# A fused convolution and linear-attention kernel: seven of nine spectral pieces summed by accumulating transfers, epsilon added elementwise, and a new order

## The chip, the cores and the metric

The kernel runs on one core of a Trainium2 chip. The metric is the device time of one execution in microseconds. A core has a tensor engine (TensorE, PE in the profile; its weight loads are PEld), a vector engine (VectorE, DVE), a scalar engine (ScalarE, ACT), GpSimd (POOL) and a queue engine (SyncE, SP) that here only issues transfers. Each engine takes its own instructions in order and waits on semaphores for the others. Transfers run on 16 DMA engines.

## What is computed

Two independent halves, joined along the channels: 2048 positions, 576 channels each.

```python
def _A_ref(q, k, v, shift_k, ssm_k, ssm_D):
    ...
    for t in range(ks):
        k_shift = k_shift + k_pad[:, t:t + S, :] * shift_k[:, ks - 1 - t][None, None, :]
    kv = k_shift * v
    ...
    y_f = kv_f * kf_f[None, :, :, :]
    ...
    y = y + kv * ssm_D[None, None, :]
    return q * y

def _B_ref(x, wqkv, wo):
    ...
    phi = lambda t: jnp.where(t > 0, t + 1, jnp.exp(t)) + 1e-6
    pq, pk = phi(q), phi(k)
    kv = jnp.einsum("bhsd,bhse->bhde", pk, v)
    z = jnp.einsum("bhsd->bhd", pk)
    num = jnp.einsum("bhqd,bhde->bhqe", pq, kv)
    den = jnp.einsum("bhqd,bhd->bhq", pq, z)[..., None] + 1e-6
    o = num / den
    return (lambda x, *d: x.transpose(*d))(o, 0, 2, 1, 3).reshape(B, S, D) @ wo
```

Half A is a short convolution of `k` with four taps, a product with `v`, a long convolution of each channel with its own filter over a transform of 4096 points, and a product with `q`. Half B is linear attention with 32 heads of 18 channels. `phi` is 1e-6 plus a positive function, and that epsilon is the one the change is about.

## The kernel before

**Half A.** The transform is taken in two steps, as matmuls with tables. The channels are cut in three chunks of 192 (`cc`), each of these in three pieces of 64, so there are nine pieces `g`. The filter goes through `h_piece`, `s1` and `s2` first and leaves a spectrum `sph` for each piece, the data (`conv_piece`: `tap`, `tap+`, `tapv`) goes through the same steps and leaves `spu`. In such a tile the partitions alternate between real and imaginary parts: even rows real, odd rows imaginary.

`inv(g, su)` multiplies the two spectra and takes the first inverse step. Two transfers on SP bring the filter's spectrum into `X` with real and imaginary rows swapped. DVE (POOL for one piece) forms two elementwise products, `p2` = `spu` x `X` and `p1` = `spu` x `sph`, in place. These are the four partial products of a complex multiplication, not yet summed. TensorE sums them: for each group `hh` of four channel quads it runs eight 128x128 matmuls at L551, four with `sph` and one table, four with `X` and another, both into the same accumulation. One 128x512 eviction (`i1ev`, to the tile `V`) follows for each group; there are four groups to a piece. `inv2(gi)` takes the second inverse step for three pieces at a time (L576) and multiplies by `q`, either after an eviction to `yb` or straight from PSUM (`i2q`), and stores the result.

**Half B.** `kproj` (L623) and `qproj` (L644) project; `phi` without its epsilon is formed by ACT's exponential and one DVE pass. `b_G` (L673) contracts the keys with the inputs, then come `kv` (L708) and `b_M` (L770), which folds the output weights in. The denominators (`den`, L744 and L748) are inverted, written to DRAM and read back spread over rows (`rb`), and `pqn` multiplies `pqT` by them in place. `b_out` (L813) gives the output. The epsilon that belongs in `phi(q)` is handled by an extra row: `msf` (L798) sums `M` over the rows of each head, times epsilon, into the spare rows 96 to 127 of the last chunk of `M`; two transfers `rh` put the inverse denominators in the same rows of `pqT`.

**The order** of all operations is written out by hand in `PLAN`: a letter for the engine (P TensorE, A ACT, D DVE, G POOL, S SP) and the number of the operation in the order in which the program records them. `PLACES` gives every buffer its address. So each engine's queue is fixed. Operations marked `two` have two tensors in SBUF as input; one of them on POOL is given a wait on the last one on DVE that stands before it in `PLAN`:

```python
            if o.info.get("two"):
                if o.eng == "DVE":
                    last = ins
                elif last is not None:
                    tc.add_manual_dep(ins, last.name, mybir.DependencyInfo(mybir.DependencyClass.Sync, mybir.DependencyReason.SCHED_ONLY),
                                      reason="products of VectorE and GpSimd one after the other")
```

The copy helper has the lines L229 (ACT), L231 (DVE) and L233 (POOL), the two-tensor helper is L236, and SP's transfers are L222.

Of the kernel before, what the change touches and what calls it, by code (L numbers as in the profile page):

```python
# [13 lines left out]
S = 2048  # L14
D = 576
# [9 lines left out]
HDT = []  # L25
ACC = [(0, 1), (2, 1)]
# [88 lines left out]
def _tables():  # L115
# [11 lines left out]
    E = np.empty((128, 32 + 2, 128), np.float32)  # L127
# [3 lines left out]
    W = np.zeros((32, 3, 32), np.float32)  # L131
    for bb in range(16):
        for k1 in range(16):
# [5 lines left out]
            W[16 + bb, 0, 2 * k1 + 1] = c  # L139
            W[2 * k1, 1, 2 * bb] = c  # L140
# [8 lines left out]
    for i in range(2):  # L149
        E[:, 32 + i, :] = np.kron(np.eye(4), W[:, 1 + i, :])  # L150

# [17 lines left out]
    C[:, o:o + 8] = EPS  # L169
# [14 lines left out]
def kernel(  # L184
# [49 lines left out]

    def tt(e, o, a, b, op):
        return (nc.vector if e == "DVE" else nc.gpsimd).tensor_tensor(out=o, in0=a, in1=b, op=op)  # L236
# [10 lines left out]
    Esb = SB("Esb", [128, 34, 128], side=1)  # L247
# [31 lines left out]
    for f in range(2):  # L279
        P.op("G", lambda e, f=f: nc.gpsimd.memset(pqT[f].t[64:128, 4, :], 0.0), wr=[(pqT[f], (4, g)) for g in (2 * f, 2 * f + 1)] + [(pqT[f], "r")], name="pqz", ms=1024, st="pqz%d" % f)  # L280
# [4 lines left out]
    load("cst", cst, lambda e: dma(e, cst.t[:], C_d), 256 * Ct.shape[1], 1612)  # L285
    load("srow", srow, lambda e: dma(e, srow.t[:], A_shift_k.rearrange("(p d) j -> p d j", p=64)), 4608, 72, engs=EARLY)
# [4 lines left out]
    load("Esb", Esb, lambda e: dma(e, Esb.t[:].rearrange("p a c -> p (a c)"), E_d), 1114112, 8704)  # L291
# [194 lines left out]
    def s2(C, cc, pp, nm):  # L486
# [23 lines left out]
        for kh in range(4):  # L510
            ps = psb(1, "s2ps")

            def mm(e, kh=kh, ps=ps):
                for j in range(4):
                    nc.tensor.matmul(  # L515
                        ps.t[32 * j:32 * j + 32, 0, :],
                        lhsT=W2()[32 * kh:32 * kh + 32, :], rhs=ct.t[32 * kh:32 * kh + 32, 8 * j:8 * j + 8],
                        start=True, stop=True)
            P.op("P", mm, rd=[ct, idw], wr=[ps], name="s2" + nm, st=st, mm=[(512, 32, 32)] * 4)
            P.op("AD", lambda e, kh=kh, ps=ps: copy(  # L520
                e, view(sp.t[:], 32 * kh, [[256, 8], [128, 2], [1, 32]]), ps.t[:, 0, :].rearrange("p (w k t) -> p w t k", w=8, t=2)),
                 rd=[ps], wr=[(sp, kh)], name="s2ev" + nm, n=512, st=st)
# [134 lines left out]
    for g in range(4):  # L657
        for c in range(5):
            qproj(c, g)
# [295 lines left out]
```

## Time and profile before

| what | us |
|---|---|
| median of 3 runs | 160.37 (159.92 to 160.57) |
| profiled execution, first to last instruction (span) | 158.3 |
| TensorE busy | 149.8 |
| DVE busy | 141.8 |
| ACT busy | 125.1 |
| POOL busy | 59.6 |

Of the profiled execution the page gives the span alone, not a time of its own; the median run is 2.07 us above it. A table of stretches has, per row, the stretch, its length, and for each engine in the order PE, PEld, DVE, ACT, POOL the busy time and the number of instructions; then the granted TensorE clock, the DMA engines' busy share and GB/s. A group of instructions has the line, engine, operation, output and inputs, shapes and count, then the busy time and the mean duration of one, then idle time before. A row of the chain of waits or of a timeline begins with its start and its length in us. A row of waits has who waited, for whom, the us in total, the number of times and the longest.

### The profile page before, as it was taken

To read this page: it belongs to the slowest core of one execution; us is meant where nothing else is said; L and a number is where in the kernel's file an instruction comes from. 1 tells how busy PE (TensorE), PEld (TensorE's weight loads), DVE (VectorE), ACT (ScalarE), POOL (GpSimd) and SP (SyncE) were. 2 spreads that over 40 slices of the span, in tenths; PEclk is the share of its full clock that TensorE was granted. 3 is DMA by queue.
4 is the path that set the end of the run, shared out by engine and by line. 5 is a ranking of instruction groups with operands and counts; after the bars stand their busy time and mean duration, and the time that the engine had idled before them with its cause. 6 is when DMAs were issued, how large, how long until landed. Compare 5 with 4: busy or idle time off the path is not lost.

```text
span 158.3 us, 4158 instructions
## 1 busy us (share of the span) xinstructions
PE 149.8 (95%) x1663; PEld 118.6 (75%) x1663; DVE 141.8 (90%) x170; ACT 125.1 (79%) x229; POOL 59.6 (38%) x53
## 2 busy tenths in 40 slices
PE   6899999999999999999999999999999999999960
PEld 2478885535679888788888887877767799999960
DVE  1547999999999998999999999999989999999690
ACT  4038999999996566467559699999899999998760
POOL 8801310011163554603611999799290000001520
PEclk9999999999999999999999999999999999999997
DMA  5999939999999809965546867881463599405766
GB/s 146 283 384 313 245 79 299 284 187 239 352 384 259 299 15 333 377 270 103 99 131 214 159 149 209 312 288 63 178 232 112 173 331 361 143 4 147 188 181 160
DMA packets 26317, 34.37 MB, mean 217 GB/s; under 512 B 15802, under 2 KB 20923, under 8 KB 25530
## 3 DMA queue, kind: packets, MB, share of 16 engines
q1 hardware_dynamic: 25754, 32.54, 66.6%
q0 software_dynamic: 544, 1.57, 5.6%
q8 instruction: 13, 0.21, 0.7%
q14 instruction: 6, 0.05, 0.1%
HBM read 20.86 MB, written 4.99 MB: 163 GB/s over the span
## 4 chain that ended last, share of the span: by engine, by line
PE 78%; ACT 8%; DVE 6%; DMA 2%; issue 1%; SPq 1%; DVEq 0%; ACTq 0%
PE ps_all L813 13%; PE ps_all L623 12%; PE ps_all L673 12%; PE ps_all L644 11%; PE ps_all L467 8%; PE ps_all L551 8%; PE ps_all L515 5%; ACT sph L229 3%; PE ps_all L576 3%; ACT V L229 3%; DMA x_sb<-in_B_x_dram 2%; PE ps_all L436 2%; DVE Ch L231 2%; ACT yb L229 1%; PE ps_all L708 1%
## 5 line engine op out<-in xcount | busy, mean ns | idle before, releaser
L644 PE MATMUL ps_all<-xT,wq 128*126 128x512 bf16 (+1 forms) x100 | 23.8, 381 | 0.1
L813 PE MATMUL ps_all<-M,pqT 126*128 126x288 bf16 (+1 forms) x160 | 22.5, 287 | 0.0
L623 PE MATMUL ps_all<-wk,xT 128*128 128x288 bf16 x160 | 20.4, 286 | 0.4 <-DVE xT L231 0.4
L402 DVE TENSOR_TENSOR m<-kh,Wj 128x6144 bf16<-128x6144 bf16 x6 | 20.1, 3349 | 0.0
L229 ACT ACTIVATE Cu<-ps_all 128x768 bf16<-128x768 f32 x22 | 17.3, 856 | 3.2 <-PE ps_all L467 3.2
L623 PEld LDWEIGHTS <-xT 128*128 128x128 bf16 x160 | 17.4, 110 | 3.1 <-DVE xT L231 0.6
L236 POOL TENSOR_TENSOR pqT<-pqT,rb 126x1024 bf16<-126x1024 bf16 (+1 forms) x9 | 19.1, 2174 | 1.0 <-DVE v L236 1.0
L813 PEld LDWEIGHTS <-pqT 126*128 126x128 bf16 (+1 forms) x160 | 16.6, 110 | 3.7 <-issue 1.9
L644 PEld LDWEIGHTS <-wq 128*126 128x126 bf16 (+1 forms) x100 | 12.5, 131 | 8.7 <-issue 2.2
L229 ACT ACTIVATE V<-ps_all 128x512 bf16<-128x512 f32 x32 | 17.2, 624 | 1.8 <-PE ps_all L551 1.8
L628 ACT ACTIVATE ek<-ps_all,neg 128x576 bf16<-128x576 f32 x16 | 11.9, 743 | 8.3 <-PE ps_all L623 8.3
L467 PEld LDWEIGHTS <-Gsb 128*128 128x128 bf16 x192 | 16.1, 98 | 2.6 <-issue 1.6
L551 PE MATMUL ps_all<-Esb,sph 128*128 128x128 bf16 x144 | 17.9, 219 | 0.1
L551 PE MATMUL ps_all<-Esb,X 128*128 128x128 bf16 x144 | 17.9, 219 | 0.0
L236 POOL TENSOR_TENSOR m<-m 128x1536 bf16<-128x1536 bf16 x4 | 12.4, 3096 | 13.1 <-DVE m L236 8.9
L673 PE MATMUL ps_all<-pk,x_sb 128*128 128x289 bf16 (+1 forms) x128 | 17.1, 287 | 0.0
L229 ACT ACTIVATE sph<-ps_all 128x512 bf16<-128x512 f32 x30 | 16.6, 608 | 0.2
L229 ACT ACTIVATE Ch<-ps_all 128x768 bf16<-128x768 f32 x19 | 15.2, 853 | 1.0 <-PE ps_all L467 0.8
L229 ACT ACTIVATE spu<-ps_all 128x512 bf16<-128x512 f32 x28 | 15.1, 613 | 0.6 <-PE ps_all L515 0.6
L236 POOL TENSOR_TENSOR q<-yb,q 128x384 bf16<-128x384 bf16 x4 | 3.6, 912 | 29.4 <-DVE yb L231 27.6
L673 PEld LDWEIGHTS <-x_sb 128*128 128x128 bf16 x128 | 12.3, 98 | 2.9
L551 PEld LDWEIGHTS <-sph 128*128 128x128 bf16 x144 | 14.0, 98 | 0.5 <-DVE sph L236 0.2
(96 smaller groups left out, 301.9 us busy)
## 6 DMA issues: line engine op xcount, KB each, us to landing
X<-sph SPq DMA_DIRECT2D x18, 256.0 KB
v<-in_A_v_dram SPq DMA_DIRECT2D x2, 1152.0 KB
out_dram<-ob SPq DMA_DIRECT2D x16, 144.0 KB
q<-in_A_q_dram SPq DMA_DIRECT2D x1, 2304.0 KB
out_dram<-q SPq DMA_DIRECT2D x12, 192.0 KB
rb<-r_scr SPq DMA_DIRECT2D x8, 252.0 KB
x_sb<-in_B_x_dram SPq DMA_DIRECT2D x3, 576.0 KB
kh<-in_A_k_dram SPq DMA_DIRECT2D x1, 1584.0 KB
```

Source lines behind the costliest of these rows:

```text
L229: nc.scalar.activation(out=o, in_=i, func=ACTF.Copy)
L236: return (nc.vector if e == "DVE" else nc.gpsimd).tensor_tensor(out=o, in0=a, in1=b, op=op)
L402: return nc.vector.tensor_tensor(out=m.t[:], in0=i0, in1=i1, op=ALU.mult)
L467: nc.tensor.matmul(ps.t[:, bank, lo - 384 * bank:hi - 384 * bank], lhsT=Gsb.t[:, b, ri, :], rhs=src[:, lo - CC * j:hi - CC * j], start=Tru ...
L515: nc.tensor.matmul(ps.t[32 * j:32 * j + 32, 0, :], lhsT=W2()[32 * kh:32 * kh + 32, :], rhs=ct.t[32 * kh:32 * kh + 32, 8 * j:8 * j + 8], st ...
L551: nc.tensor.matmul(ps.t[:, 0, 128 * c:128 * c + 128], lhsT=src.t[:, 4 * hh + c, :], rhs=Esb.t[:, 32 + wi, :], start=(wi == 0), stop=(wi == 1))
L576: nc.tensor.matmul(ps.t[:, 0, n * j:n * j + n], lhsT=Esb.t[:, 2 * b + ri, :], rhs=V[gi].t[:, 2 * b + ri, :], start=(ri == 0), stop=(ri == 1))
L623: nc.tensor.matmul(ps.t[:, hh, 0:HALF], lhsT=cols(xT.t[0:KT[t], t, :], r), rhs=wk.t[0:KT[t], t, HALF * hh:HALF * hh + HALF], start=(t == 0 ...
L628: P.op("A", lambda e: nc.scalar.activation(out=eb.t[:], in_=ps.t[:, :, 0:HALF], func=ACTF.Exp, bias=neg1.t[:]), rd=[ps, neg1], wr=[eb], na ...
L644: nc.tensor.matmul(ps.t[0:hn, 0, :], lhsT=wq.t[0:KT[t], t, h0:h0 + hn], rhs=xT.t[0:KT[t], t, :], start=(t == 0), stop=(t == 4))
L673: nc.tensor.matmul(ps.t[0:m, 0, 0:n], lhsT=x4[r // 4].t[:, r % 4, :] if t == 4 else x_sb[r // 4].t[:, r % 4, 128 * t:128 * t + 128], rhs=p ...
L813: nc.tensor.matmul(ps.t[:, 0, 0:HALF], lhsT=cols(pqT[r // 8].t[0:kn, c, 512 * (r // 4 % 2):512 * (r // 4 % 2) + 512], r), rhs=M.t[0:kn, c, ...
```

## The change

In seven of the nine pieces (`ZA`) the sum of the four partial products is formed before TensorE sees them. `X` now gets the odd (imaginary) rows of `sph` in all rows, and a third transfer fills the odd rows of `sph` with its even ones. POOL multiplies `X` by a column of signs, -1 and +1 by turns (`sgn`). After the two products, two transfers issued by POOL add `X`, rows swapped, into `sph` (`zacc`, accumulating). A quad then needs one matmul instead of two. Pieces 7 and 8 stay as they were.

In half B the extra rows, `msf`, its copy, `rh` and their memsets are gone. Instead epsilon is added to every element of `pqT` (`pqe`) after the denominators have been formed and before `pqn`.

The last two groups of the second three pieces in `inv2` (`gi == 1 and bg >= 6`) take the other way to the product with `q`, with a store each. `PLAN` and `PLACES` are new throughout. The options `MS2`, `MI1`, `MO`, `MQ` and `ZP` are off or empty, and the code for them does what it did.

```diff
+ZP = []
+ZA = [0, 1, 2, 3, 4, 5, 6]
+NW = 1 if len(ZP) + len(ZA) == 9 else 3
+MS2, MI1, MO, MQ = False, False, False, False
...
+    C[0::2, o + 4] = -1.0
+    C[1::2, o + 4] = 1.0
+    C[:, o + 5] = -C[:, o + 4]
...
+    def scale(e, o, a, c):
+        if e == "ACT":
+            nc.scalar.activation(out=o, in_=a, func=ACTF.Copy, scale=c)
+        else:
+            (nc.vector if e == "DVE" else nc.gpsimd).tensor_scalar(out=o, in0=a, scalar1=c, scalar2=None, op0=ALU.mult)
...
+        z, za = g in ZP or g in ZA, g in ZA
         for i in range(2):
-            load("X", xb, lambda e, i=i: dma(e, xb.t[i:128:2], tx.t[1 - i:128:2]), 262144, 4096, rd=[tx], wr=[(xb, i)])
+            load("X", xb, lambda e, i=i: dma(e, xb.t[i:128:2], tx.t[(1 if z else 1 - i):128:2]), 262144, 4096, rd=[tx], wr=[(xb, i)])
+        if z:
+            load("X", tx, lambda e: dma(e, tx.t[1:128:2], tx.t[0:128:2]), 262144, 4096, wr=[tx])
...
+        if z:
+            P.op("GDA", lambda e: scale(e, xb.t[:], xb.t[:], sgn.t[:, int(za):int(za) + 1]), rd=[sgn], wr=[xb], name="sgn", n=2048, st=st)
...
+        if za:
+            for i in range(2):
+                load("zacc", tx, lambda e, i=i: nc.gpsimd.dma_start(out=tx.t[i:128:2], in_=xb.t[1 - i:128:2], accum_op=ALU.add),
+                     262144, 4096, rd=[xb], wr=[(tx, 2 * i), (tx, 2 * i + 1)], engs="G")
...
+                        for wi, src in ((0, tx),) if z else ((1, tx), (2, xb)):
+                            nc.tensor.matmul(ps.t[:, hh, 128 * c:128 * c + 128], lhsT=src.t[:, 4 * (h0 + hh) + c, :], rhs=Esb.t[:, 32 + wi, :],
+                                             start=(wi < 2), stop=(wi != 1))
...
+            ya = gi in YA and not (gi == 1 and bg >= 6)
...
+            P.op("DG", lambda e, c=c, hn=hn, f=f: (nc.vector if e == "DVE" else nc.gpsimd).tensor_scalar(
+                out=pqT[f].t[0:hn, c, :], in0=pqT[f].t[0:hn, c, :], scalar1=EPS, scalar2=None, op0=ALU.add),
+                 wr=[(pqT[f], (c, g)) for g in (2 * f, 2 * f + 1)], name="pqe", n=1024)
...
-        load("rh", None, lambda e, f=f: dma(e, pqT[f].t[96:128, 4, :], ap(r_d, 1024 * f, [[2 * S, 32], [1, 1024]])), 65536, 2048,
-             rd=[(rtok, (f, 0))], wr=[(pqT[f], "r")])
-    P.op("G", lambda e: nc.gpsimd.memset(M.t[64:128, 4, :], 0.0), wr=[(M, 4), (M, "s")], name="Mz", ms=576)
...
-    P.op("P", smm, rd=[(M, c) for c in range(5)] + [cst], wr=[sps], name="msf", mm=[(288, 126, 128)] * 10)
...
```

In the new order the engines of some operations differ too:

| operations | before | after |
|---|---|---|
| `sgn` | none | POOL 7 |
| `zacc` | none | POOL 14 |
| `pqe` | none | POOL 9, DVE 1 |
| `pqn` | POOL 9, DVE 1 | POOL 8, DVE 2 |
| `tap+` | DVE 6, POOL 4 | DVE 8, POOL 2 |
| `i1ev` | ACT 32, DVE 4 | ACT 29, DVE 7 |
| `oev` | ACT 22, DVE 10 | ACT 25, DVE 7 |
| `X` on SP | 18 | 25 |

On POOL the seven sign passes stand apart: piece 3's among the convolution's products, pieces 5 and 0 among and after `pqn`, piece 4's after that, then six `zacc` (pieces 3, 5, 4), the sign passes of pieces 6, 2 and 1, and eight `zacc` (pieces 6, 2, 1, 0).

More of the change, by code (lines that the diff above doesn't have):

```diff
@@ L246 @@
     Gsb = SB("Gsb", [128, 16, 2, 128], side=1)
-    Esb = SB("Esb", [128, 34, 128], side=1)
+    Esb = SB("Esb", [128, 32 + NW, 128], side=1)
+    sgn = SB("sgn", [128, 2], FP32, side=1)
     srow = SB("srow", [64, D // 64, 4])
@@ L657 @@
     for g in range(4):
-        for c in range(5):
-            qproj(c, g)
+        for c, m in ((0, 2), (2, 2), (4, 1)) if MQ else [(c, 1) for c in range(5)]:
+            qproj(c, m, g)
     GT = SB("GT", [128, 5, D])
```

213 lines of the change are left out of this document (109 added, 104 removed), and 32 rows, old and new, of the table PLACES.

## The prediction

> **What bounds the kernel now.** I read the page's busy shares first, then TensorE's own waits, then a table of stretches, then the chain that ended last.
>
> ```profile
> PE 149.8 (95%) x1663; PEld 118.6 (75%) x1663; DVE 141.8 (90%) x170; ACT 125.1 (79%) x229; POOL 59.6 (38%) x53
> PE 78%; ACT 8%; DVE 6%; DMA 2%; issue 1%; SPq 1%; DVEq 0%; ACTq 0%
> ```
> ```profile
> PE ps_all L844 <- DVE cft L840: 1.5, 1, 1.5
> PE ps_all L323 <- DVE x L231: 0.5, 1, 0.5
> PE ps_all L623 <- DVE xT L231: 0.4, 1, 0.4
> ```
> ```profile
> 75.00:100.00 25.00, 24.73 (x256) 20.46 (x254) 24.60 (x27) 19.95 (x33) 16.39 (x8) 1.00 0.65 167
> 100.00:124.00 24.00, 24.00 (x317) 17.78 (x317) 22.68 (x32) 22.91 (x50) 14.61 (x6) 1.00 0.53 187
> 124.00:150.00 26.00, 25.92 (x400) 24.93 (x392) 24.55 (x31) 23.83 (x52) 2.65 (x3) 1.00 0.59 196
> ```
>
> TensorE is busy for 149.8 of 158.3 us, at the full granted clock in these stretches (1.00, the column before the DMA share), and every wait it has lies in the first microseconds. From 75 us to 150 us it has no gap to speak of, so matmul time taken away there is time taken off, until another engine is late. The busy columns are PE, PEld, DVE, ACT, POOL: DVE and ACT run within 1 to 2 us of TensorE in the last two stretches. Only POOL and the DMA engines have room (2.65 of 26 us; share 0.53 to 0.59). So the question is which engine is late next.
>
> The span is 158.3 us; the median of the runs is 160.37. I make the sum on the span and carry the difference, 2.07 us, over.
>
> **What TensorE loses.** Two rows of the chain and the two groups give the price.
>
> ```profile
> 99.58 1.30 PE ps_all L798 x10
> 128.60 2.68 PE ps_all L551 x48
> ```
> ```profile
> L551 PE MATMUL ps_all<-Esb,sph 128*128 128x128 bf16 x144 | 17.9, 219 | 0.1
> L551 PE MATMUL ps_all<-Esb,X 128*128 128x128 bf16 x144 | 17.9, 219 | 0.0
> ```
>
> Matmuls are pipelined, so the mean of 219 ns is not what one occupies: 48 in a row take 2.68 us, 55.8 ns each. Each piece has 16 on `sph` and 16 on `X`; seven pieces lose the 16 on `X`: 112 x 0.0558 = 6.25 us. The ten matmuls of the epsilon row (L798) go too: 1.30 us, with a copy, two small transfers and three memsets behind them that hold nothing up. Together 7.55 us: the span would be 150.75 us, a run 152.8.
>
> **What ACT and DVE have.** The new order moves a net eight copies onto ACT. The costliest form is the 128x768 eviction, so at most 8 x 0.86 = 6.9 us over the whole span:
>
> ```profile
> L229 ACT ACTIVATE Cu<-ps_all 128x768 bf16<-128x768 f32 x22 | 17.3, 856 | 3.2 <-PE ps_all L467 3.2
> ```
>
> From 100 to 150 us ACT is already busy for 22.91 + 23.83 = 46.7 of 50 us, and the change takes no eviction away: a quad of the inverse still needs its whole copy. If nothing moved between the stretches, ACT alone would let these 50 us shrink by only 3.3, to a run of 157.1. I take that as a cross-check, not a term, since the order may move copies into ACT's free 5 us before 100. DVE has eight instructions fewer and is not the bound unless it is held up (second rival).
>
> **What POOL gets.** Per piece a pass over `X` by a column of signs (`sgn`, 2048 elements, one tensor in) and two accumulating transfers (`zacc`, 256 KB each); ten passes that add epsilon to `pqT` (`pqe`, 1024 elements), nine on POOL. None of these is in the trace. The nearest rows:
>
> ```profile
> L280 POOL MEMSET pqT<- 64x1024 bf16 x2 | 1.9, 947 | 0.1
> L277 POOL MEMSET x<- 128x256 bf16 x4 | 1.2, 305 | 0.1
> L233 POOL COPY x<-x_sb 128x256 bf16<-128x256 bf16 x1 | 0.4, 395 | 0.0
> L236 POOL TENSOR_TENSOR pqT<-pqT,rb 126x1024 bf16<-126x1024 bf16 x7 | 15.0, 2172 | 1.0 <-DVE v L236 1.0
> L236 POOL TENSOR_TENSOR X<-spu,X 128x2048 bf16<-128x2048 bf16 x1 | 4.1, 4074 | 2.8 <-DVE spu L231 2.8
> L407 POOL DMA_DIRECT2D m<-m x2 | 2.5, 1274 | 12.2 <-DVE m L402 6.7 <-DVE zsel L729 5.5
> ```
> ```profile
> DMA to landing us min/median/max: 6.4/6.5/6.5
> ```
> ```profile
> q0 software_dynamic: 272, 0.79, 44.3%
> ```
> ```profile
> 103.14 0.35 SPq L222 DMA_DIRECT2D Esb<-tab_e  x1
> ```
>
> A pass with one input lies between a memset (0.95 us for 1024 elements) and one with two inputs (2.17 us; 4.07 for 2048). It is nearest to the copy, 395 against 305 ns for the memset of that size, 1.3 times: 0.95 to 1.23 us for `pqe`, 1.9 to 2.45 for `sgn`. I take 1.1 and 2.15. The Trainium skill (GPSIMD Engine Reference, 3.1 Elementwise — side-by-side cycle accounting) has a short loop body bound at 1.03 cycles per element of a 1.2 GHz clock; by that estimate `sgn` is 1.8 us and the chain below 2.1 us shorter; no row here shows it.
>
> Issuing an accumulating transfer of 768 KB held POOL for 1.27 us; SP issues a plain one in 0.35. `zacc` is a third of that size: 0.35 to 1.34, taken 0.9. It landed 6.5 us after issue; the queue's 0.79 MB took 44.3% of a 10 us stretch, 4.43 us of all engines, so 2.1 us are fixed and 256 KB takes 1.48: landing after 3.6 us, with 6.5 as the other end.
>
> **Whether POOL keeps up.** POOL and TensorE run in order, and in the new order both can be counted between two places: the end of the denominators (`den`), which frees `pqT` for `pqe`, and the inverse matmuls of piece 1, which wait for its `zacc`. POOL has 9 `pqe`, 1 `acc`, 8 `pqn`, 6 `sgn`, 1 product and 12 `zacc`: 9.9 + 1.27 + 17.4 + 12.9 + 4.07 + 10.8 = 56.3, and 3.6 to land: 59.9 us. For TensorE:
>
> ```profile
> 79.66 1.98 PE ps_all L673 x16
> 81.64 0.33 PE ps_all L467 x4
> 93.92 1.39 PE ps_all L708 x25
> 97.92 0.65 PE ps_all L770 x4
> 112.42 0.99 PE ps_all L515 x28
> 127.98 0.62 PE ps_all L813 x5
> 142.39 0.33 PE ps_all L576 x4
> ```
>
> 7 groups of L673 (13.9), 22 of L467 (7.3), 48 of L515 at four matmuls (6.8), L708 (1.4), 5 of L770 at two (1.6), 26 of L813 (16.1), inverse quads 17 x 4 and 8 x 8 matmuls (7.4), 7 of L576 (2.3): 56.8 us. POOL is late by 3.1 us, and TensorE stalls by it at the last pieces: everything behind, the output matmuls woven in among them included, waits in TensorE's queue. With the lower ends POOL needs 50.5 us and nothing is late; with the copy's rate, 1.34 and 6.5 it needs 71.2 and is 14.4 late; with two-input rates 89, which the copy row speaks against.
>
> SP's seven extra `X` transfers (the third of a piece must wait until the first two have read the tile, and what is behind it on SP waits too: output stores and `q`) are apart from their pair in the order; at nothing, as the loads run a stage ahead.
>
> **The transfers themselves.**
>
> ```profile
> q1 hardware_dynamic: 1531, 3.96, 54.6%
> 126.34 0.39 SPq L222 DMA_DIRECT2D q<-in_A_q_dram  x1
> ```
>
> The first row is of 120 to 140 us: 3.96 MB in 10.9 us of all engines, 363 GB/s. From 100 to 150 us the engines are used for 0.53 x 24 + 0.59 x 26 = 28 us. The change adds 14 x 1.48 = 20.7 and 7 x 0.72 = 5: 54 in 50 us. The 2.36 MB of `q` alone, 6.5 us, come in amid the `zacc`. So a `zacc` will at times be served by halves; between 0 and 6.5 us, taken 1.9.
>
> **Sum:** 158.3 - 7.55 + 3.1 + 1.9 = 155.75; with 2.07, 157.8 us. The start of the new order is dealt differently, but the same loads come first, and its end has one more product straight out of PSUM and one more store, with DVE off the chain there for most of it: 0 for both, give or take 1. Two sums of the convolution come from POOL to DVE, whose eight fewer instructions pay for them.
>
> **Rivals.** (1) *All of it is hidden.* POOL at its lower ends: 152.8. ACT's 46.7 of 50 us speak against. 10%.
>
> (2) *POOL's one-input passes and DVE's two-tensor passes shut each other out.* The trace keeps the two kinds apart:
>
> ```profile
> 57.22 3.12 POOL L236 TENSOR_TENSOR v<-m,v 128x1536 bf16<-128x1536 bf16 x1 [3.71 <-DVE m L402]
> 97.85 2.12 POOL L236 TENSOR_TENSOR pqT<-pqT,rb 126x1024 bf16<-126x1024 bf16 x1
> ```
> ```profile
> 60.79 1.75 DVE L236 TENSOR_TENSOR m<-m 128x3072 bf16<-128x3072 bf16 x1
> 99.95 0.95 DVE L236 TENSOR_TENSOR v<-m,v 128x1536 bf16<-128x1536 bf16 x1
> 118.86 1.22 DVE L236 TENSOR_TENSOR sph<-spu,sph 128x2048 bf16<-128x2048 bf16 x1
> ```
>
> The two POOL passes end at 60.34 and 99.97, where DVE's begin; in the code they carry a mark (`two`), which `sgn` and `pqe` lack. So no row shows them side by side. If they exclude each other, six `sgn` meet DVE's products (1.22 us) and five `pqe` its conv passes; meeting halfway, 6 x 0.6 = 3.6 and about 3.3 more on POOL's late chain: 161.4 to 164.7, say 163. It decides from 3.4 us on. 27%. The Trainium skill (SBUF — State Buffer, Who interferes with whom) states just this: a VectorE instruction with two SBUF inputs contends with a GpSimd instruction that reads SBUF, and the second one blocks; with it the sum is this rival's.
>
> (3) *POOL is slow*: 14.4 us late: 158.3 - 7.55 + 14.4 + 2.07 = 167.2. 13%.
>
> (4) *Given back*: POOL's and the transfers' lateness adds to about 7.5, and the time stays at 160.4. 13%.
>
> **How the numbers follow.** 157.8 has 37% (155.5 to 159.5). What differs by under 0.5% from 160.37 a measurement of this kernel can't tell from no change. Faster: 37 + 10 = 47%; same 13%; slower 27 + 13 = 40%. The range reaches from just above the first rival to short of the third: 153.5 to 166. The forecast's own is 155.5 to 159.5, as cases of both signs hold much of the chance.
>
> **What would show it.** L551's successor down to 176 matmuls and TensorE busy near 142 us; `sgn` near 2.15 us and `pqe` near 1.1; TensorE waiting for DMA `sph` in the last 30 us, about 5 us in all (right), or for nothing (first rival). DVE passes on `sph` and `X` longer than 1.22 us, or POOL passes of twice their shortest, show the second. I am wrong in kind if ACT stands where I have POOL.

## The result, and the profile after

| | before | after |
|---|---|---|
| time, median | 160.30 us | 206.22 us (204.57 to 208.83, 4 runs); 205.99 of the three compared |
| profiled execution, its span | 158.3 us | 202.5 us |
| granted clock, mean | 0.994 | 0.898 |

Some executions of one and the same kernel take over 1.5% longer than its fastest; the ratios and the comparisons below leave these out, and the table of experiments has the medians with and without them.

The ratio is 1.2831 (95% interval 1.2776 to 1.2886): some 46 us slower. The prediction said 157.8 us, in a range of 153.5 to 166. It was wrong in direction and far outside its range.

The page of the changed kernel: busy time by engine, the granted clock in 40 slices, and the group of the epsilon passes (busy time in all, mean ns of one; the last column says what the engine waited for):

```profile
PE 156.6 (77%) x1541; PEld 117.0 (58%) x1541; DVE 160.4 (79%) x164; ACT 127.8 (63%) x237; POOL 131.8 (65%) x79
PEclk9999999999999999999995555855799999599999
...
L821 POOL TENSOR_SCALAR pqT<-pqT 126x1024 bf16<-126x1024 bf16 (+1 forms) x9 | 28.6, 3179 | 2.9 <-PE ps_all L788 2.3
```

TensorE was forecast near 142 us. It has 122 matmuls fewer than before and is busy for 6.8 us more, because for a good part of the second half its clock is granted at 0.5: the same matmuls take longer. And it idles for 46 us, where before it idled for 8.5. POOL has gone from 59.6 to 131.8 us. The groups apart by shape:

```profile
L250 POOL TENSOR_SCALAR X<-X,sgn 128x2048 bf16<-128x2048 bf16 x7 | 40.8, 5843 | 1.1 <-PE ps_all L810 1.1
L253 POOL TENSOR_TENSOR pqT<-pqT,rb 126x1024 bf16<-126x1024 bf16 x6 | 13.6, 2277 | 1.2 <-issue 1.2
L576 POOL DMA_DIRECT2D sph<-X x14 | 12.3, 1190 | 2.7 <-DVE X L253 1.4 <-issue 1.3
L253 DVE TENSOR_TENSOR X<-spu,X 128x2048 bf16<-128x2048 bf16 x8 | 19.5, 2441 | 0.3 <-POOL X L250 0.3
L589 PE MATMUL ps_all<-Esb,sph 128*128 128x128 bf16 x144 | 13.9, 229 | 12.3 <-DVE ob L242 7.0 <-issue 2.7 <-ACT ob L240 1.1
L589 PE MATMUL ps_all<-Esb,X 128*128 128x128 bf16 x32 | 5.7, 265 | 0.0
```
```profile
DMA to landing us min/median/max: 3.7/6.0/8.6
```

`sgn` takes 5.84 us (forecast 2.15), `pqe` 3.18 (forecast 1.1): POOL's new work is 28.6 + 40.8 + 12.3 = 81.7 us, where the forecast's prices make 37.5. All of the difference is in the passes: issuing the transfers took 12.3 us, forecast 14 x 0.9 = 12.6. An accumulating transfer lands 6.0 us after its issue (forecast 3.6). The mean of VectorE's products on `X` has doubled from 1.21 to 2.44 us, and the mean hides how. Their shortest, median and longest, in ns:

```profile
L253 DVE TENSOR_TENSOR X<-spu,X x8: 1211/1221/4727, 148.5 to 178.9; 128x2048 bf16<-128x2048 bf16 x8
```

Most take 1.22 us as before; three, which lie beside POOL's sign passes, take 4.3 to 4.7. The 144 + 32 inverse matmuls are the 176 forecast. Where the waits went (engine and line, what it waited for, us in all, times, the longest):

```profile
PE ps_all L484 <- DVE v L253: 20.1, 1, 20.1
DVE ct L523 <- POOL pqT L253: 14.4, 1, 14.4
PE ps_all L589 <- DVE ob L242: 7.0, 3, 3.4
```

One wait of TensorE is 20.1 us long. The second row tells whose it is: VectorE stands for POOL. POOL's own timeline (start, length, what):

```profile
79.44 29.18 POOL L821 TENSOR_SCALAR pqT<-pqT 126x1024 bf16<-126x1024 bf16 x9 [2.34 <-PE ps_all L788]
108.68 1.23 POOL L424 DMA_DIRECT2D m<-m  x1
...
156.01 18.59 POOL L250 TENSOR_SCALAR X<-X,sgn 128x2048 bf16<-128x2048 bf16 x3
174.56 5.29 POOL L576 DMA_DIRECT2D sph<-X  x6
180.44 1.73 POOL L576 DMA_DIRECT2D sph<-X  x2 [0.59 <-DVE X L253]
```

From 79.44, where the prediction's chain begins, to piece 1's `zacc` at 179.85 us POOL has hardly a gap: 100.4 us, 4.4 of them idle, for which the forecast had 56.3. The stretches (busy columns PE, PEld, DVE, ACT, POOL; then the clock, the DMA share, GB/s):

```profile
100.00:104.00 4.00, 2.62 (x26) 1.95 (x24) 0.00 (x0) 3.65 (x6) 3.86 (x3) 1.00 0.42 120
104.00:125.00 21.00, 2.24 (x15) 1.45 (x15) 10.83 (x7) 1.32 (x2) 19.64 (x9) 0.56 0.54 152
125.00:150.00 25.00, 24.00 (x250) 12.35 (x249) 19.24 (x24) 18.99 (x38) 23.17 (x7) 0.69 0.63 234
150.00:180.00 30.00, 20.89 (x235) 17.27 (x234) 29.50 (x21) 18.20 (x42) 28.51 (x15) 0.89 0.80 221
```

From 104 to 125 us POOL is busy almost throughout, VectorE for half of it, TensorE and ACT hardly at all. In the next 25 us TensorE looks fully busy, but at a clock of 0.69. Of the chain that ended last (start, length, what), three pieces stand out:

```profile
163.87 4.30 DVE X L253
...
169.66 4.29 DVE X L253
...
177.53 6.80 DMA sph<-X
```

The first two are held products on `X`; VectorE's evictions `ob`, for which TensorE waits 7.0 us in all, come behind them in its queue. The third is the landing of an accumulating transfer.

### The profile page after: what moved, and what is told of

Read it like the earlier page. It is cut to its first block, busy times and chain, and to the rows that moved or that the text cites. A ratio compares the mean times of both kernels' runs of the same rounds, so it can differ in the third digit from the quotient of the medians.

```text
span 202.5 us, 3962 instructions
## 1 busy us (share of the span) xinstructions
PE 156.6 (77%) x1541; PEld 117.0 (58%) x1541; DVE 160.4 (79%) x164; ACT 127.8 (63%) x237; POOL 131.8 (65%) x79
## 3 DMA queue, kind: packets, MB, share of 16 engines
q0 software_dynamic: 1664, 5.24, 14.1%
## 5 line engine op out<-in xcount | busy, mean ns | idle before, releaser
L250 POOL TENSOR_SCALAR X<-X,sgn 128x2048 bf16<-128x2048 bf16 x7 | 40.8, 5843 | 1.1 <-PE ps_all L810 1.1
L240 ACT ACTIVATE Cu<-ps_all 128x768 bf16<-128x768 f32 x23 | 18.4, 848 | 23.4 <-PE ps_all L484 21.6
L821 POOL TENSOR_SCALAR pqT<-pqT 126x1024 bf16<-126x1024 bf16 (+1 forms) x9 | 28.6, 3179 | 2.9 <-PE ps_all L788 2.3
L484 PE MATMUL ps_all<-v,Gsb 128*128 128x192 bf16 x96 | 11.2, 265 | 21.4 <-DVE v L253 20.1
L841 PE MATMUL ps_all<-M,pqT 126*128 126x288 bf16 (+1 forms) x160 | 25.5, 309 | 0.1
L589 PE MATMUL ps_all<-Esb,sph 128*128 128x128 bf16 x144 | 13.9, 229 | 12.3 <-DVE ob L242 7.0
L419 DVE TENSOR_TENSOR m<-kh,Wj 128x6144 bf16<-128x6144 bf16 x6 | 22.8, 3818 | 0.1
L523 DVE STREAM_TRANSPOSE ct<-Cu 128x1024 f32<-128x1024 f32 x9 | 10.7, 1220 | 14.4 <-POOL pqT L253 14.4
L841 PEld LDWEIGHTS <-pqT 126*128 126x128 bf16 (+1 forms) x160 | 17.1, 114 | 6.5 <-issue 3.3
L253 DVE TENSOR_TENSOR X<-spu,X 128x2048 bf16<-128x2048 bf16 x8 | 19.5, 2441 | 0.3 <-POOL X L250 0.3
L253 POOL TENSOR_TENSOR hT<-hT,Drow 1x64 bf16<-1x64 bf16 (+2 forms) x5 | 1.7, 342 | 27.5 <-DVE hT L242 10.3
L240 ACT ACTIVATE spu<-ps_all 128x512 bf16<-128x512 f32 x30 | 17.3, 621 | 2.8 <-PE ps_all L534 2.1
L253 POOL TENSOR_TENSOR pqT<-pqT,rb 126x1024 bf16<-126x1024 bf16 (+1 forms) x8 | 17.2, 2297 | 1.2 <-issue 1.2
L713 PE MATMUL ps_all<-pk,x_sb 128*128 128x289 bf16 (+1 forms) x128 | 17.1, 287 | 0.0
```

Of the source, the lines that this page charges most:

```text
L240: nc.scalar.activation(out=o, in_=i, func=ACTF.Copy)
L250: (nc.vector if e == "DVE" else nc.gpsimd).tensor_scalar(out=o, in0=a, scalar1=c, scalar2=None, op0=ALU.mult)
L419: return nc.vector.tensor_tensor(out=m.t[:], in0=i0, in1=i1, op=ALU.mult)
L484: nc.tensor.matmul(ps.t[:, bank, lo - 384 * bank:hi - 384 * bank], lhsT=Gsb.t[:, b, ri, :], rhs=src[:, lo - CC * j:hi - CC * j], start=Tru ...
L589: nc.tensor.matmul(ps.t[:, hh, 128 * c:128 * c + 128], lhsT=src.t[:, 4 * (h0 + hh) + c, :], rhs=Esb.t[:, 32 + wi, :], start=(wi < 2), stop ...
L713: nc.tensor.matmul(ps.t[0:m, 0, 0:n], lhsT=x4[r // 4].t[:, r % 4, :] if t == 4 else x_sb[r // 4].t[:, r % 4, 128 * t:128 * t + 128], rhs=p ...
```

## The experiments

Four things could hold the 46 us: POOL's passes, their meeting with VectorE's, the transfers of the sums, and the new order itself. The measured times in one table: the median of all 4 to 6 runs (one run for e1 and e2), then the median of the runs compared. The expectations name the first.

| run | base | edit | us, all runs | us, compared |
|---|---|---|---|---|
| e1 | after | `pqe` on VectorE | 195.95 (one run) | |
| e2 | after | `sgn` on VectorE | 197.56 (one run) | |
| e3 | after | both | 184.49 | 182.65 |
| e4 | after | neither pass at all | 178.35 | 178.18 |
| e5 | e3 | no `zacc` | 175.09 | 173.64 |
| e6 | e5 | no third copy of X | 175.19 | 174.22 |
| e7 | e3 | old sums | 174.60 | 174.60 |
| e8 | e3 | 26 idle matmuls | 182.98 | 180.70 |
| e9 | after | `acc` earlier | 208.03 | 208.03 |
| e10 | before | epsilon elementwise on VectorE | 169.84 | 169.70 |
| e11 | before | new sums | 198.69 | 193.50 (one run) |
| e12 | e7 | no `pqe` | 174.63 | 174.27 |
| e13 | after | a buffer freed earlier | 205.86 | 205.86 |
| e14 | e7 | 26 idle matmuls | 172.54 | 171.91 |
| e15 | before | as e10, placed earlier | 164.75 | 164.75 |
| e16 | e12 | `wv` loaded earlier | 172.87 | 172.40 |
| e17 | e16 | 21 idle matmuls | 182.83 | 182.00 |

### The passes on POOL: e1, e2, e3, p1

A letter of the order names an engine: G is POOL, D is VectorE. e1 changes it for the nine `pqe`, e2 for the seven `sgn`, e3 for all sixteen.

```diff
-... D265 G264 P211 A212 D70 A213 P494 G267 G241 ...
+... D265 D264 P211 A212 D70 A213 P494 D267 D241 ...
```

> The changed kernel with its nine epsilon passes on DVE instead of POOL, at the same places of the order; nothing else is moved. Theory A (a pass of one input on POOL is simply long, 2.77 us for 1024 elements, and what is queued behind it on POOL comes late): 9 x 2.77 = 25 us leave POOL's queue ahead of the second `acc`, TensorE's wait of 20 us for the convolution goes, and the time falls to 175 to 183 us. Theory B (POOL's passes are of the length I forecast, and the time goes into POOL and DVE shutting each other out): only the 3.7 us that these passes are longer than their shortest and what DVE loses beside them come back, 193 to 198 us. Theory C (the accumulating transfers are what is late): no change here, above 200.

> The changed kernel with its seven sign passes on DVE instead of POOL; the epsilon passes stay on POOL. Theory A: the stall of 20 us behind the epsilon passes stays, the 6 x 5.44 us of signs in POOL's queue go: 183 to 190 us. Theory B: DVE's products on `X`, longer by 9.8 us in all, come back to 1.21 us each, 194 to 198 us. Theory C: `zacc` lands 6.0 us after issue as before and TensorE still waits for it at the last pieces, above 200.

> Both kinds of passes on DVE, POOL keeps the transfers, `pqn` and its sums. Theory A and B: no one-input pass is left on POOL, and the time is that of my sum without POOL's lateness plus 7 to 10 us more work on DVE: 156 to 164 us. Theory C: TensorE waits for `sph` by transfer in the last pieces, 170 us or more.

195.95 and 197.56 lie in B's ranges, 184.49 (ratio 1.1367, 1.1328 to 1.1406) in C's. The two gains, 10.0 and 8.4, add to 18.4, and together they give 23.3. So POOL's passes are some 23 us of the loss, and 22 are left that none of the three names rightly. The two profiles bear out a part of A and a part of B: TensorE's wait for `v` is 4.5 us in e1 and 17.1 in e2, as A has it, and in e2 all products on `X` are back at 1.22 us, as B has it.

p1 measures single passes, one at a time and then two engines side by side; it computes nothing of the kernel, and its output is zeros. POOL's copies and passes with an immediate number have VectorE's memsets beside them; its pass by a column and its products run with VectorE idle.

```text
POOL alone: copy; tensor_scalar (immediate, column); tensor_tensor
DVE alone: tensor_scalar (column); tensor_tensor
together: POOL 3 tensor_scalar || DVE 12 products
          POOL 2 copies || DVE 6 products
          POOL 2 tensor_scalar || DVE 8 tensor_scalar
```

> None of the reference's work: the output is zeros, and one pass of each kind runs by itself and then beside a pass of the other engine. Alone on POOL, 128 partitions. Theory A: a multiply or an add by one number takes 2.7 ns per element alone (5.4 us for 2048, 2.8 for 1024), a copy 1.2 ns (2.4 us) and a two-input product 2.0 ns (4.07). Theory B: the multiply takes 2.1 us alone and 5 only beside DVE's products. Both: a DVE product that starts beside a POOL pass takes up to that pass's length instead of 1.2 us if the two exclude each other, 1.2 us if they do not. The sign pass on DVE should take 0.6 to 1.2 us, on ACT 1.7 to 2.1.

Its timeline, POOL first, then VectorE; all of 2048 elements:

```profile
8.75 1.89 POOL L46 COPY b<-a 128x2048 bf16<-128x2048 bf16 x1
23.04 5.44 POOL L49 TENSOR_SCALAR b<-a,col 128x2048 bf16<-128x2048 bf16 x1 [4.09 <-DVE colb L41]
28.56 4.04 POOL L50 TENSOR_TENSOR b<-a,c 128x2048 bf16<-128x2048 bf16 x1
32.69 3.60 POOL L51 TENSOR_TENSOR b<-a,colb 128x2048 bf16<-128x2048 bf16 x1
...
45.75 6.46 POOL L60 TENSOR_SCALAR e<-c,col 128x2048 bf16<-128x2048 bf16 x1 [9.47 <-ACT c L58]
...
58.21 5.82 POOL L62 TENSOR_SCALAR e<-c,col 128x2048 bf16<-128x2048 bf16 x1
...
82.10 5.86 POOL L73 TENSOR_SCALAR l<-k 128x2048 bf16<-128x2048 bf16 x1 [5.03 <-DVE k L72]
88.05 5.67 POOL L74 TENSOR_SCALAR l<-k 128x2048 bf16<-128x2048 bf16 x1
```
```profile
36.32 0.75 DVE L53 TENSOR_SCALAR d<-b,col 128x2048 bf16<-128x2048 bf16 x1 [13.45 <-POOL b L51]
37.57 1.23 DVE L55 TENSOR_TENSOR d<-d,b 128x2048 bf16<-128x2048 bf16 x1
45.68 25.25 DVE L64 TENSOR_TENSOR f<-c,g 128x2048 bf16<-128x2048 bf16 x12 [4.50 <-ACT c L58]
82.04 15.87 DVE L76 TENSOR_SCALAR f<-k 128x2048 bf16<-128x2048 bf16 x8
```

A sign pass alone on POOL takes 5.44 us, more than a product of two tensors (4.04) and nearly three times a copy (1.89). Written as a product with a column spread over the row (L51) it took 3.60. VectorE does the pass in 0.75. So theory A is right about the length. The meeting is real, too: twelve products that take 12 x 1.23 = 14.8 us alone took 25.25 beside three POOL passes, so they lost 10.5 us to passes that last 6.46 + 2 x 5.82 = 18.1. They were not all slowed: nine took their own 1.23 us, and three, one beside each POOL pass, 4.62. Beside two copies on POOL (2.95 and 2.77 us in place of 1.89) six products took 10.66 us in place of 7.4. Eight fast one-input passes, some 6 us alone, took 15.87, and 4.2 of these lie behind the end of POOL's second pass at 93.72: hardly more than two got through beside POOL's two. How the 23 us divide between the passes' length and the meeting, no run separates.

### TensorE's wait of 20 us: e9, e13

The first reading was POOL's queue: the convolution's second accumulating transfer (`acc`, whose product was ready at 91.8 us) stood behind the `pqe` until 108.68. e9 moves that one word.

```diff
-G244 D83 G250 G261 G247 G270 G258 S259 G84 ...
+G244 D83 G84 G250 G261 G247 G270 G258 S259 ...
```

> The new kernel (206.2 us) with one word of the order moved: the second accumulating transfer of the convolution (acc) goes to POOL ahead of five of the passes that add epsilon instead of behind them, right behind the product that it sums. All the passes stay on POOL. Theory Q (TensorE's wait of 20 us at 104 to 124 us is POOL's queue: the transfer was ready at 92 us and issued at 108.7): issued at 92 to 95 us, the wait shrinks to under 8 us, and the time falls to 190 to 198 us. Rival (POOL's sum of work sets the end, wherever the transfer stands): 203 to 208 us.

It was issued at 95.52, and nothing was gained: 208.03 us, TensorE's wait 20.3. VectorE's timeline in e9 shows why:

```profile
99.79 1.22 DVE L523 STREAM_TRANSPOSE ct<-Ch 128x1024 f32<-128x1024 f32 x1
115.32 1.25 DVE L523 STREAM_TRANSPOSE ct<-Cu 128x1024 f32<-128x1024 f32 x1 [14.30 <-POOL pqT L253]
116.48 5.39 DVE L253 TENSOR_TENSOR m<-m 128x1536 bf16<-128x1536 bf16 x1
```

A transpose of the convolution's spectrum has no data from `pqT`. What it waits for is memory: its output `ct` is placed over two `rb` tiles, which POOL's normalisations (`pqn`) still have to read, and those stand behind POOL's `pqe`. The convolution's sum (L253 on `m`) is next in VectorE's queue and takes 5.39 us in place of 0.92, beside POOL's sign pass. e13 lets POOL do the two `pqn` in question first, with their `pqe`, and `acc` ahead of them; nothing is added.

```diff
-P494 G267 G241 A495 ... G244 D83 G250 G261 G247 G270 G258 S259 G84 ... G263 ... G272 G260
+P494 G267 G261 G270 A495 ... D83 G84 G263 G272 G241 G244 G250 G247 G258 S259 ... G260
```

> The new kernel (206.2 us) with POOL's passes in another order, none added or taken away: the two normalisations whose reciprocals (rb) lie where VectorE's next transpose (ct) is to be written, and their two epsilon passes, go ahead of the other five epsilon passes, and the second accumulating transfer of the convolution ahead of them. Theory B (TensorE's wait of 20 us is this buffer: VectorE stood 14.3 us for POOL's pass on pqT): VectorE's wait shrinks to under 3 us and TensorE's to under 8 us, and the time falls to 193 to 201 us. Rival (POOL's sum of work sets the end, so the wait moves on): VectorE's wait shrinks, and the time is 203 to 209 us.

That wait of VectorE is gone, and the time is the same, 205.86: the rival. The waits of e13:

```profile
ACT spu L240 <- POOL pqT L253: 17.4, 2, 16.8
PE ps_all L534 <- ACT spu L240: 12.1, 1, 12.1
```

Now ACT stands for POOL, and TensorE for ACT. In the changed kernel, in e9 and in e13 POOL is busy almost without a gap from 80 to 182 us (187 in e9), and the three end within 2.2 us of each other, wherever the wait stands. That fits POOL's sum of work as what sets the end in these three. It does not hold for e2: there POOL has gaps of up to 7.1 us, TensorE's wait of 17.1 us stays, and only 8.4 us are gained.

### The transfers of the sums: e4, e5, e6, e7

Each leaves operations out where they are issued:

```diff
+            if o.name in ('zacc',):
+                continue
             ins = o.fn(o.eng)
```

e4 names `sgn` and `pqe` (base: the changed kernel), e5 `zacc` (base: e3), e6 also the third X transfer, e7 these and `sgn`. In e7 the two `X` transfers swap rows as before, and the inverse does two matmuls per quad again, both on `sph`, so that it does not wait for `X`.

> The new kernel without the seven sign passes and without the ten passes that add epsilon (the signs and the epsilon are missing from the outputs); the accumulating transfers, the copies of X, the order and everything else stay. Beside the run with both passes on VectorE (184.5 us) it takes 9 us of work off VectorE and nothing else. Theory T (what is left above the kernel before is the transfers: 14 accumulating ones and 7 more copies on the DMA engines, and SP's queue behind them): 178 to 184 us. Theory O (the new order itself, timed for other durations, costs it): 178 to 184 us as well. Theory D (VectorE, which got the 9 us, is what is late): 165 to 174 us. Were the two kinds of passes all of it, it would be 153 to 158.

> Both passes on VectorE (184.5 us), and the 14 accumulating transfers left out: the inverse matmuls read the product on sph alone, so the sum's second half is missing from the output. POOL issues no such transfer and nobody waits for one. Theory T: 158 to 168 us. Theory O: 176 us or more. Theory D: 176 us or more.

> As the one before, and the seven extra copies inside sph (the third transfer of a piece, behind which SP's queue stands) left out too: the products on sph are of wrong rows. It tells what of the transfers' cost is the copies'. Theory T: 2 to 8 us below the run without the accumulating transfers, that is 153 to 160 us. Theory O: no change against it.

> The new order with the old kind of sums: no accumulating transfer, no extra copy, no sign pass; the inverse does two matmuls per channel quad again (of the seven pieces' products the one on sph is read twice, so TensorE has its 112 matmuls back but does not wait for X, and the sums are not the right ones); epsilon is added elementwise on VectorE. What it takes above the kernel before is the order's and the epsilon's. Theory T: 157 to 162 us. Theory O: 170 us or more.

e5 is 9.0 us below e3: that is what the accumulating transfers cost here. The third copies cost nothing that shows (174.22 against 173.64). A stretch of e3, then of e5, shows the DMA engines (share in the second last column; executions of 185.28 and 176.00 us):

```profile
124.00:150.00 26.00, 23.73 (x234) 15.33 (x231) 22.28 (x24) 20.62 (x48) 9.55 (x9) 0.83 0.94 291
```
```profile
124.00:150.00 26.00, 25.27 (x290) 17.49 (x275) 24.17 (x28) 22.61 (x53) 3.19 (x1) 0.90 0.71 272
```

In e3 their share is 0.94 for 26 us, where the kernel before had 0.59. But e5, e6 and e7 did not come near the 153 to 168 us of theory T: all stop at 174 to 175. e5 lies below O's and D's ranges by 0.9 us, e6 and e7 in O's. In e7 the seven pieces' 112 matmuls are back, while seven sign passes (8.6 us on VectorE in e3) and the third copies are gone, and the time is within 1.0 us of e5's. So what the change saves on TensorE buys nothing here against what it adds; what the matmuls alone are worth, no run separates. e4, in the range that T and O share, is 4.5 us below e3 for some 11 us less work on VectorE (138.7 us busy against 150.1).

### The new order: e8, e10, e12, e14 to e17

e12 leaves out `pqe` as well. It is the new order with the old work less the epsilon row. "The order" stands here for all that comes with it: the new places of the buffers, the engines of the copies and products, the two groups of `inv2`.

> The new order with the old kind of sums (174.6 us), and the ten epsilon passes left out as well (epsilon is missing from the output): what is left is the new order alone, with the kernel before's work less the epsilon row. Theory O (the order is late by itself): 168 to 174 us. Theory E (it is the epsilon passes on VectorE, which cost 9.5 us in the old order too: 169.8 against 160.1): 158 to 164 us.

174.63 us (174.27), 14.1 above the kernel before (160.17 beside it): just above theory O's range and far from E's. TensorE is busy there for 157.7 us, 7.9 more than before with ten matmuls fewer, and idle for 15.9 us, 7.4 more. Its stretches, with the clock third from the end of each row:

```profile
100.00:104.00 4.00, 0.87 (x11) 0.41 (x8) 3.08 (x3) 1.32 (x2) 1.68 (x1) 0.76 0.85 256
104.00:108.00 4.00, 3.02 (x41) 2.75 (x46) 0.00 (x0) 1.31 (x2) 2.40 (x2) 0.50 0.96 245
108.00:112.00 4.00, 3.19 (x46) 1.15 (x25) 3.22 (x6) 3.23 (x7) 1.46 (x2) 0.89 0.74 239
112.00:116.00 4.00, 4.00 (x42) 1.56 (x39) 3.70 (x6) 3.46 (x7) 4.00 (x3) 0.54 0.93 343
116.00:120.00 4.00, 4.00 (x36) 1.52 (x35) 4.00 (x6) 2.78 (x6) 2.90 (x2) 0.50 0.89 312
120.00:124.00 4.00, 4.00 (x28) 2.00 (x27) 2.04 (x3) 2.58 (x6) 2.16 (x1) 0.50 0.75 299
```
```profile
PE ps_all L748 <- DMA wv<-in_B_wqkv_dram: 4.1, 1, 4.1
```

In the old order TensorE had work for all of these microseconds. Here it first waits (0.8 us for VectorE's `v`, 4.1 for `wv`, whose load SP issues behind the second half's reciprocals), and then runs at half the clock for most of the next 20 us. Which of the two costs the time, four runs tried to tell. e8 (base e3) and e14 (base e7) put idle matmuls ahead of the groups that wait, 8 + 10 + 8 = 26 of them (the expectations say 24):

```diff
+            for i in range({721: 8, 713: 10, 226: 8}.get(o.id, 0)):
+                nc.tensor.matmul(psall[:, 7, :], lhsT=ident(), rhs=Gsb.t[:, 0:2]..., start=True, stop=True)
             ins = o.fn(o.eng)
```

> The kernel with both passes on VectorE (184.5 us) with 24 idle matmuls of 512 columns added, into a free bank of PSUM: 8, 10 and 6 of them ahead of the three matmul groups between 103 and 109.5 us for which TensorE stood waiting, some 5 us of work in all at the full clock. They compute nothing that is used. Theory G (the wait of 6 us is dear because the granted clock falls to 0.50 after it and stays there for 20 us): the clock stays at 1.00 behind the place, and the time falls to 174 to 179 us although TensorE has more to do. Rival (the wait costs only its own length, and what comes behind it is set by transfers and VectorE): no lower than before, 184 to 190 us.

> The new order with the old kind of sums (174.6 us) and the 24 idle matmuls at the three places. With both passes on VectorE and the transfers in place the idle matmuls kept the clock at 0.98 and gave only 1.5 us; here no accumulating transfer stands behind them. Theory G (the low clock costs where TensorE sets the end): clock above 0.98 and 164 to 169 us. Rival (the low clock is paid in time in which TensorE would wait anyway): 173 to 177 us.

In e8 the clock stayed at 1.00 from 100 to 124 us (mean of the run 0.981), and the time fell by 2.0 us only (ratio 1.1294, 1.1241 to 1.1346; the interval overlaps e3's), between the two expectations. The idle matmuls themselves take 6.0 us of TensorE. That beside the transfers the low clock is paid in time that would be waited anyway fits this, but is not shown. In e14's profiled execution, its longest (175.93 us), the clock fell after all, only later (0.50 from 116 to 124 us). The three others, at mean clocks of 0.990, 0.990 and 0.967, took 171.91, 170.92 and 173.16 us. So with the clock nearly kept the order takes some 3 us less than e7 (174.60; clocks of 0.917 to 0.931), although it carries the 6.0 us of idle matmuls, and is still some 11 us above the kernel before. e16 takes away the wait for `wv`, and e17 adds idle matmuls to it, behind the place too.

```diff
-D238 S257 D69 ... D682 S222 P226
+D238 S222 S257 D69 ... D682 P226
```

> The new order alone (old sums, no epsilon: 174.6 us) with one word moved: the load of wv goes to SP ahead of the first half's reciprocals (about 80 us) instead of behind the second half's (issued at 99.5, landed at 104.4, TensorE standing 4.1 us for it). Theory W (the order is late here because of SP's queue, and the low clock of 0.50 from 102 to 126 us comes of that wait): the wait for wv is gone, the clock stays at 1.00 and the time falls to 160 to 166 us. Only the wait and not the clock: 169 to 172 us. Rival (what wv hid is as late: VectorE's v and the matmuls of 32 columns behind it): 173 to 176 us.

> As the one before, with 21 idle matmuls of 512 columns in free banks: 10 ahead of the two groups where TensorE waits at 98 to 106 us, and one ahead of each of eleven groups behind them, where it runs its matmuls on 32 rows and 32 columns, in which the clock of the run with 24 idle matmuls fell to 0.50 after all (113 to 126 us). Theory G (the low clock is what the new order loses here): clock 0.98 or more, and 160 to 166 us. Rival (the clock stays up, but TensorE then waits for VectorE, ACT or transfers, as beside the accumulating transfers): 169 to 175 us.

e16: 172.87, so the wait goes and the time follows by 1.9 us (the intervals of the two ratios overlap); the clock still falls, to 0.54 and 0.50 from 108 to 120 us. e17 is spoilt: its idle matmuls themselves stood 3.3 us for ACT's evictions out of the bank that they use, and the clock fell as before (0.50 from 112 to 132 us), 182.83. So of the 14 us of the order, the runs attribute some 2 to SP's queue and some 3 to the low clock, which may be in part the same; what the rest is stays open.

e10 and e15 put the epsilon alone into the old order, five passes per half on VectorE, and leave out the epsilon row: in e10 ahead of each load of reciprocals, in e15 right behind the half's reciprocal.

```diff
+                for c, (h0, hn) in enumerate(HCH):
+                    nc.vector.tensor_scalar(out=pqT[f].t[0:hn, c, :], in0=pqT[f].t[0:hn, c, :], scalar1=EPS, scalar2=None, op0=ALU.add)
```

> The kernel before, in its own order, with epsilon added elementwise: ten passes on VectorE of 0.34 us ahead of the ten loads of the reciprocals, and without the epsilon row's ten matmuls, its eviction, its two small transfers and its three memsets. If the elementwise epsilon as such costs nothing on VectorE: 158.5 to 160.5 us. If VectorE's 3.4 us come out behind TensorE, with a low clock after it: 163 to 168 us; then part of what the run of the old sums (174.6 us) has above the kernel before is the epsilon's, and not the order's.

> The kernel before, in its own order, with epsilon added elementwise on VectorE as in the run that took 169.8 us, but all five passes of a half right behind that half's reciprocal (76 to 83 us), before POOL's first normalisation at 87 us. Theory X (a fast one-input pass on VectorE is shut out by POOL's passes: one of 0.38 us took 5.04): no such pass over 0.6 us, and 158.5 to 163 us. Rival (VectorE has no 3.4 us to give, wherever they stand): 166 to 172 us.

e10 took 169.84 us (169.70), 9.6 more than the kernel before (160.06 beside it) for some 3.4 us of passes, above both expectations. VectorE in e10, then POOL in e10:

```profile
91.70 0.38 DVE L782 TENSOR_SCALAR pqT<-pqT 126x1024 bf16<-126x1024 bf16 x1
...
94.71 5.04 DVE L782 TENSOR_SCALAR pqT<-pqT 126x1024 bf16<-126x1024 bf16 x1
```
```profile
92.21 4.22 POOL L236 TENSOR_TENSOR pqT<-pqT,rb 126x1024 bf16<-126x1024 bf16 x2 [2.00 <-PE ps_all L673]
96.38 3.08 POOL L236 TENSOR_TENSOR m<-m 128x1536 bf16<-128x1536 bf16 x1
```

A pass that takes 0.38 us alone lasted until POOL's row of products had ended at 99.46. In e15 the first half's five took 3.36 us (the tail of a product on POOL still lay beside them), the second half's, with POOL idle, 1.69; the time is 164.75 (ratio 1.0284, 1.0249 to 1.0318), between the two expectations. 4.6 us more for 5.05 us of passes: VectorE has nothing to give there in the old order, and the epsilon row that the change removed (1.30 us of matmuls) was the cheaper way in it.

### The new sums in the old order: e11

The third copy, the sign pass on VectorE, the two accumulating transfers and the single matmul, all put into the kernel before at the places of their products:

```diff
+            if za and done[1] == 2:
+                for i in range(2):
+                    nc.gpsimd.dma_start(out=tx.t[i:128:2], in_=xb.t[1 - i:128:2], accum_op=ALU.add)
```

> The kernel before, in its own order, with the new sums for seven pieces: the third copy behind the second on SP, the sign pass on VectorE ahead of its product, the two accumulating transfers on POOL right behind the later of the two products, one inverse matmul per quad (with the first of the two old matrices, so these sums are not the right ones). Epsilon stays as before. Theory X (the transfers of the sums cost about 9 us wherever they stand, as the runs with and without them did: 184.5 against 175.1): 163 to 172 us. Theory O (the sums cost little; it is the new order that is late): 153 to 160 us. Slower than the new order's 184.5 would say that the sums need an order of their own.

198.69 us, in runs that differ by 4% (193.5 to 201.5): beyond both theories. TensorE's first row of waits in e11:

```profile
PE ps_all L574 <- DMA sph<-X: 17.8, 4, 6.3
```

Four waits of up to 6.3 us for landings, which the old order leaves no time for. So the sums need an order of their own, and the new one is better for them by some 11 us (e3, both by the runs compared); in neither do they pay: e3 is 8 us above e7.

## Why the prediction was wrong

The runs make a chain from one kernel to the other: the new order alone +14.1 (e12), epsilon on VectorE +0.3 (e7), new sums with signs on VectorE and without the accumulating transfers -1.0 (e5), those transfers +9.0 (e3), both passes from VectorE to POOL +23.3 (the changed kernel). The steps add up by construction, and each has its size in this sequence only: the epsilon that costs 0.3 in the new order costs 9.6 in the old one (e10), and the sums that cost 8 here cost some 33 there (e11). By the prediction's own steps:

- **What POOL gets.** This is the step that failed first: "It is nearest to the copy". The forecast chose between a copy and a two-input product and took the row of a 128x256 copy. A one-input pass with a scalar is at neither end: alone it is 1.35 times the product, outside the bounds of 1.9 to 4.07. In the changed kernel the chain from `den` to piece 1's `zacc` is 29.2 (nine `pqe`) + 1.2 + 17.2 (eight `pqn`) + 35.4 (six `sgn`) + 4.1 + 10.5 (twelve `zacc`) = 97.6 us in rows that overlap a little, 100.4 from end to end, and 6.0 to land. The forecast had 56.3 and 3.6, and set aside 89 as what "the copy row speaks against". The Trainium skill's figure (GPSIMD Engine Reference, 3.1 Elementwise — side-by-side cycle accounting), 1.03 cycles per element, gave an estimate of 1.8 us for `sgn`; the measured 5.44 us are 3.2 cycles of that clock, and the measurement decides.
- **Whether POOL keeps up.** The form of the step, POOL's sum against TensorE's, fits: by 100.4 + 6.0 against 56.8 POOL is 49.6 us late, and the forecast's own sum with 49.6 for 3.1 gives 204.3 us. This estimate comes so near to 206.2 partly by luck, since the order is late by itself (e12) and TensorE's 56.8 us are at the full clock.
- **The second rival** is real, and was given 27%. Three products of VectorE took 4.3 to 4.7 us beside POOL's sign passes in the changed kernel, and in p1 twelve lost 10.5 us to 18.1 us of such passes. Its price (3.6 + 3.3 us) was made with `sgn` at 2.15 us. The Trainium skill (SBUF — State Buffer, Who interferes with whom) has a fast one-input pass of VectorE blocked in full by a GpSimd pass: e10's 5.04 us for 0.38 agree. For a product of two tensors it speaks of contention; in p1 nine of twelve such products took their own time, and three were held to 4.62 us.
- **The transfers.** Taken 1.9 us, measured 9.0. The landing of 3.6 us came from splitting a landing of 6.5 us into a fixed part and a rate; the median is 6.0 for a third of the size, beside 6.4 and 9.3 for the two transfers of 768 KB in the changed kernel. No run shows that fixed part and rate. SP's seven extra copies, costed at nothing, cost nothing that shows (e6).
- **The start and end of the new order**, "0 for both, give or take 1". This is the second step that failed: the order alone costs 14.1 us. The prediction counted what the order issues and not when: it looked for what is late at `den` and `zacc` but not at `wv`, `v` and the evictions from 96 to 126 us, where TensorE has holes and its clock falls.
- **What TensorE loses.** The matmuls were counted rightly (176), but the 7.55 us did not come off the time: TensorE is busy for 6.8 us more, at a mean clock of 0.898, and e7 with the 112 matmuls back and the sign passes gone is as fast as e5.
- **What would show it.** TensorE was to wait some 5 us for transfers into `sph` in the last 30 us; the chain that ended last has such a landing (6.8 us), but the long waits are for `v` (20.1) and `ob` (7.0). The named sign of the second rival, products on `X` longer than 1.22 us, is there. ACT does not stand where POOL does: the kind of the bound was right, its size was not.

## What to carry to other kernels

A price for an operation that the trace does not show cannot be taken from the cheapest neighbour, and two neighbours are no bounds unless a reason puts the operation between them: here the one-input pass with a scalar was dearer than the two-input pass. When a change comes with a new order, the order is an edit with a price of its own, and the first experiment is the new order with the old work. A single long wait in a profile need not be the cause: where removing it moves the wait to another engine at the same time, look for the engine whose sum of work stands behind both. Where a mean has doubled, look at the shortest and the longest: here most passes were as fast as ever, and a few were held.

## What the hardware showed that was not expected

- POOL, 128x2048 in bfloat16: one tensor by a column of scalars 5.44 us, product of two tensors 4.04, product with a column spread over the row 3.60, each with VectorE idle; one tensor by an immediate 5.36 and copy 1.89, beside VectorE's memsets. VectorE does the pass by a column in 0.75.
- Beside POOL's one-input passes VectorE's products of two tensors are held one at a time, not slowed alike: 1.23 us or 4.62 us in p1, 1.22 or 4.3 to 4.7 in the changed kernel.
- TensorE's granted clock stayed at 0.54 to 0.50 in stretches in which it was busy 4.00 of 4 us by the profile (e12, 112 to 124 us). The Trainium skill (TensorE: Matmul & The Clock Gate, What's actually happening) gives it back after some 3.4 us of sustained work; here 12 us of it did not do so. Some 4.4 of these 12 us are matmuls on 32 rows and 32 columns; whether that matters, no run here tested.
- Fourteen accumulating transfers of 256 KB took a median of 6.0 us from issue to landing, 3.7 at the least and 8.6 at the most, where those of 768 KB took 6.4 and 6.5 in the kernel before, and 6.4 and 9.3 in the changed one.
